# DeltaNet attention followed by a quick-GELU feed-forward block: the dummy matmuls around the first hops are laid out anew, and four key norms are multiplied in by another engine

## The chip, the cores and the metric

One core of one Trainium2 chip. The metric is the device time of one execution in microseconds (us); three executions are given by their median. One further execution was profiled. PE is TensorE, DVE VectorE, ACT ScalarE, POOL GpSimd, and SP the engine that issues most DMAs.

## The reference

```
# attention: B, H, S, D = 4, 8, 768, 48
k_n = k / (norm(k) + 1e-6)
for t in range(S):
    y[t]  = q[t] @ state
    v_old = k_n[t] @ state
    state = state + beta[t] * outer(k_n[t], v[t] - v_old)
# feed-forward: x is y as (3072, 384); w_in (384, 2048), w_out (2048, 384)
h = x @ w_in
g = h / (1 + exp(-1.702 * h))
out = g @ w_out
```

## The kernel before

**Units.** The sequence is cut into six chunks of 128 positions. A unit is one chunk of one of the four batches, with its eight heads; units are numbered chunk by chunk, so that 0 to 3 are the first chunk, 4 to 7 the second and 8 to 11 the third. Within a chunk the recurrence is solved in four blocks of 32 positions. For that each unit needs its keys turned (`turn`, L443: four PE transposes into psT, evacuated to kT), their Gram product (`gram`, L417: sixteen PE instructions into psG, evacuated to G), and the inverses of the 32 by 32 diagonal blocks (`invert`, L484: a long row of small DVE products, tiles P, YB and NT). The blocks of G go to DRAM (Nd) and come back as NT (`send_blocks`, `load_diagonals`); the inverse goes out as Yd and comes back as XB.

**Hops.** `together` (L938) does one hop for a pair of units: for each head, 32-row products with XB (`solve`, into psU) and with G (`below`, into psR). ACT copies psU to US, and DVE subtracts psR from V. A hop can start its psU when V of the hop before is updated. The first pair, units 0 and 1, has eight hops (0 to 7, loop L1118); the pair 2 and 3 has eight more (hop 0 at L1132, hops 1 to 7 in the loop at L1151). Beside the hops of the first pair the keys of units 6 and 7 are turned (hops 1 and 3) and their Gram products made (hops 4 and 5).

**Outputs.** `put_out(s)` (L1112) makes a unit's outputs (psY, sixteen products), the products for the state (psS), calls `fill(1.7)`, has DVE add psS to the state (tile ST), and lets ACT copy psY to xT and last. After an odd unit six transfers on SP's queue (xT<-last) complete xT. Only then can `hidden` (L737) start: x @ w_in into ph, in two PSUM banks shared with the dummies (tag moe), each evacuated by ACT's gelu into gT. `feed` does one piece of it.

**Dummies.** `warm(n)` (L137) issues n bf16 matmuls of 128 by 128 by 256 into a bank that nobody reads (ps_warm). Their counts are NW, NR, NA, NY and NU at L59. NY of them stand at the end of the first inverse (L550), in front of hop 0. In the hops of the first pair six follow hops 0, 1 and 3 and twelve follow hop 2; none stand at hops 4 and 5, where the Gram products are. Six stand in front of `put_out` of unit 1 (L1133), and twelve follow hops 1 and 2 of the second pair.

**Background work.** The weights arrive in a wide format, and each piece is made float32 by six operations, five on DVE and one (Relu) on ACT (`conversion`, L209). `background` (L296) is one generator: conversions of w_in, then `invert(1)`, then conversions of w_out, with the cost of each step written beside it. `fill(us)` (L307) takes steps from it until the written costs come to us. A finished piece can trigger further weight loads on SP's queue (`fetches`).

**Order.** vec, act, pe, pool and sync are wrappers that pin each operation in the order of the program text, so each engine and SP's queue works in that order. After the second pair a loop of 25 (L1185) does `fill(1.0)` and `feed()` each time and, at written points, steps of `prepare_early` (L1170) for units 8 to 11. That calls `normalize_mixed` (L335): ACT squares the keys, DVE sums them (ssq), POOL takes the root (rn), DVE adds 1e-6, takes the reciprocal and multiplies the keys by it in one operation. Two steps later the keys of units 8 and 9 are turned. Then `both_written` (L883) does g @ w_out (po) as pieces of w_out become ready, woven with the later chunks (`woven`, L985).

Of the kernel before, what the change touches and what calls it, by code (L numbers as in the profile page):

```python
# [12 lines left out]
ALU = mybir.AluOpType  # L13
ACT = mybir.ActivationFunctionType
# [4 lines left out]
def kernel(  # L19
# [21 lines left out]
    B, H, S, D = q.shape  # L41
# [9 lines left out]
    NB = C // BS  # L51
# [4 lines left out]
    HF, HM = FC // 2, DM // 2  # L56

    XR = DP - D
    NW, NR, NA, NY, NU = 80, 11, 3, 28, 12  # L59
    NQ = DFF // 4  # L60
    NPC = DFF // 8
    assert S % C == 0 and H == 8 and D <= DP and DM == H * D == KC * 128
# [57 lines left out]
    vec, act, pe, pool = Engine(nc.vector), Engine(nc.scalar), Engine(nc.tensor), Engine(nc.gpsimd)  # L120
# [16 lines left out]
    def warm(n, after=None):  # L137
        ps = ps_moe.tile([128, 256], F32, tag="moe", name="ps_warm")
        if after is not None:
            after(ps[:, 0:1], 0.0)  # L140
        for _ in range(n):
            pe.matmul(ps, lhsT=ones[:, 0:128], rhs=ones, start=True, stop=True)
# [164 lines left out]
    def fill(us):  # L307
        while us > 0:
            us -= next(behind, us)
# [6 lines left out]
    def home(n):  # L316
        return KX if n in (len(KN), 3 * B - 1) else KN[n % len(KN)]
# [17 lines left out]
    def normalize_mixed(n):  # L335
        K = home(n)[:, :, 0:D]
        ksq = wk.tile([128, H, D], F32, tag="ksq", name="ksq", bufs=1)
        act.activation(ksq, K, ACT.Square)
        yield
        ssq = wk.tile([128, H], F32, tag="ssq", name="ssq", bufs=4)  # L340
        vec.tensor_reduce(ssq, ksq, axis=AX.X, op=ALU.add)
        rn = wk.tile([128, H], F32, tag="rn", name="rn", bufs=4)
        pool.tensor_tensor(rn, ssq, half, op=ALU.pow)
        yield
        vec.tensor_scalar(rn, rn, 1e-6, None, op0=ALU.add)
        vec.reciprocal(rn, rn)
        vec.tensor_tensor(K, K, rn.broadcast_to([128, H, D]), op=ALU.mult)
        yield

    def normalize_first():  # L350
# [66 lines left out]
    def gram(n):  # L417

        c, b = units[n]
        kT = kTs[n]  # L420
        G = (
            g_tile().rearrange("p f (o t) -> p (f o) t", o=2) if n < HB
            else wk.tile([128, H, 128], F32, tag="G", name="G", bufs=6)
        )
        pool_, tag = (ps_seq, "seq") if c == 0 else (ps_big, "big")
        ps = [pool_.tile([128, NP, 128], F32, tag=tag, name="psG") for _ in range(2)]
        for h in range(H):
            r = slice(h % 2 * 64, h % 2 * 64 + D)
            pe.matmul(
                ps[h % 2][:, h // 2], lhsT=kT[r, h // 2, :], rhs=kT[r, h // 2, :],  # L430
                start=True, stop=True,
            )
        act.activation(G[:, 0::2], ps[0], ACT.Copy)
        if B <= n < 2 * B + HB:
            act.activation(G[:, 1::2], ps[1], ACT.Copy)
        else:
            vec.tensor_copy(G[:, 1::2], ps[1])
        ready[n] = KN[n % len(KN)], kT, G
        return G
# [3 lines left out]
    def turn(n):  # L443
        kTs[n] = wk.tile([128, NP, 128], F32, tag="kT", name="kT", bufs=5)
        transposed(home(n), kTs[n])
# [23 lines left out]
    def send_blocks(n, others=(), dma=sync):  # L469

        G = ready[n][2]
        Nd = dram.tile([H * C * BS], F32, tag="Nd", name="Nd", bufs=4)
        to = Nd.rearrange("(h p k) -> p h k", p=C, k=BS)
        for blk in range(NB):
            u = slice(blk * BS, (blk + 1) * BS)
            (beside if blk in others else dma)(out=to[u], in_=G[u, :, u])
        return Nd
# [95 lines left out]
    def bank(name, shape=(128, H, D)):  # L573
        return ps_seq.tile(list(shape), F32, tag="seq", name=name)
# [363 lines left out]
    def together(solves, belows):  # L938

        solves = [(X, blk) for X, blk in solves if X]  # L940
        belows = [(X, blk) for X, blk in belows if X]
        psU = bank("psU") if solves else None
        psR = bank("psR") if belows else None
        for h in range(H):
            for X, blk in solves:
                X.solve(blk, h, psU)
            for X, blk in belows:
                X.below(blk, h, psR)
        for X, blk in solves:
            X.solved(blk, psU)  # L950
        for X, blk in belows:
            X.rest(blk, psR)
# [159 lines left out]
    def put_out(s):  # L1112
        s.queries()
        s.outputs(True, lambda: fill(1.7))
        steps.pop(s.n)

    path, later = hops(*pair[:2]), hops(*pair[2:])
    for i in range(2 * NB):  # L1118
        together(*next(path))
        if i in (1, 3):  # L1120
            turn(B + HB + i // 2)
        if i in (4, 5):
            gram(B + HB + i - 4)
            Ndx.append(send_blocks(B + HB + i - 4))
        elif i < 2 * NB - 2:
            warm(NU if i == 2 else NU // 2)
        if 0 < i < 2 * NB - 1:
            fill(1.7)
        if i == 2 * NB - 2:
            put_out(pair[0])  # L1130
    load_diagonals(Ndx)
    together(*next(later))  # L1132
    warm(NU // 2)  # L1133
    put_out(pair[1])
    sync(out=KN[0], in_=KX)
    load(8, ((KN, k),), sync)
# [7 lines left out]
    def feed(n=1):  # L1144
        for _ in range(n):
            while ffn and next(ffn[0], None) is None:
                ffn.pop(0)
# [2 lines left out]
    ffn.append(hidden(xTs[0], gTs[0], slice(0, NTH), 1.3))  # L1150
    for i in range(1, 2 * NB):  # L1151
        together(*next(later))
        if i > 2:
            feed()
        else:
            warm(NU)
        fill(1.7)
    for s in pair[2:]:
        put_out(s)
# [10 lines left out]
    def prepare_early(n, gram_too=True):  # L1170

        for _ in normalize_mixed(n):
            yield
        yield
        if gram_too:
            turn(n)
            yield
            gram(n)
            Nds[n] = send_blocks(n)
            yield  # L1180
# [58 lines left out]
```

## Time and profile before

| what | value |
|---|---|
| three executions | 764.84, 770.88, 770.75 us |
| their median | 770.75 us |
| the profiled execution | 771.24 us |
| its span, first to last instruction | 769.5 us |
| its mean granted PE clock | 0.964 |
| clock by the page's slices of 19.2 us, the first nine, in tenths | 9 6 7 8 6 9 9 9 8 |
| dummies, number in all | 203 |
| psU before hop 0 starts | 65.11 us |
| first ph matmul after the wait for xT | 100.81 us |

All times within an execution count from its first instruction. Busy times of PE are modelled ends of pipelined matmuls. The granted clock is a share of full speed; in this trace it is 1.0 or 0.5. All lines of the kernel's engine operations carry the line of the pinning helper, L108, so rows are told apart by their tiles.

### The profile page before, as it was taken

The numbers are of one execution on the slowest core, as the hardware profiler recorded it, in microseconds if no ns is written. First come the engines' busy times: TensorE is split into PE (matmuls) and PEld (weight loads), VectorE is DVE, ScalarE is ACT, GpSimd is POOL, SyncE is SP. The second block draws the span as 40 slices with busy tenths as digits, with TensorE's granted clock in tenths as the row PEclk, the third lists the DMA queues.
The fourth block names the chain that finished last, engine by engine and source line by source line (L and its number), as shares of the span: only waits on it lengthen the run. The fifth ranks groups of instructions, "written<-read, shape, count | busy, mean of one in ns | idle before, by whom it ended". The sixth has DMA issues, their size and how long they took to land.

```text
span 769.5 us, 19639 instructions
## 1 busy us (share of the span) xinstructions
PE 729.1 (95%) x8427; PEld 625.3 (81%) x8427; DVE 489.3 (64%) x1014; ACT 238.7 (31%) x527; POOL 242.3 (31%) x210
## 2 busy tenths in 40 slices
PE   9288999988999999999999999999999999999998
PEld 7166868855667888898988898988988988988987
DVE  4798689999777676677677777767767850110000
ACT  3363443532333422322322323322322323222120
POOL 5023001310056541542632632722711601403122
PEclk9678699989999999999999999999999999999999
DMA  9985645541223113113113123113122120000000
GB/s 170 137 165 123 175 112 78 106 117 48 59 50 81 36 28 82 37 31 80 36 32 78 36 42 71 36 41 70 36 45 56 22 55 2 2 26 2 26 0 21
DMA packets 128182, 47.11 MB, mean 61 GB/s; under 512 B 117920, under 2 KB 122144, under 8 KB 128096
## 3 DMA queue, kind: packets, MB, share of 16 engines
q1 hardware_dynamic: 125568, 41.54, 26.3%
q0 software_dynamic: 1344, 3.93, 2.3%
q8 instruction: 66, 1.08, 0.6%
q10 hardware_dynamic: 1184, 0.39, 0.2%
q14 instruction: 20, 0.16, 0.1%
HBM read 33.13 MB, written 11.01 MB: 57 GB/s over the span
## 4 chain that ended last, share of the span: by engine, by line
PE 73%; DVE 16%; issue 3%; POOL 3%; DMA 3%; SPq 1%; ACT 0%; DVEq 0%; POOLq 0%; ACTq 0%
PE ph L108 27%; PE po L108 24%; PE psY L108 6%; PE psU L108 5%; DVE P L108 4%; DVE w_out L108 3%; PE psQ L108 3%; DVE YB L108 3%; PE psG L108 2%; PE ps_warm L108 2%; PE psR L108 2%; DVE NT L108 2%; PE psT L108 2%; DVE raw L108 1%; SPq L108 1%
## 5 line engine op out<-in xcount | busy, mean ns | idle before, releaser
L108 PE MATMUL ph<-xT,w_in 128*128 128x256 f32 x1152 | 262.9, 384 | 1.6 <-DMA xT<-last 1.4
L108 PEld LDWEIGHTS ph<-xT,w_in 128*128 128x128 f32 x1152 | 215.0, 190 | 33.3 <-issue 2.5
L108 PE MATMUL po<-w_out,gT 128*128 128x192 f32 (+1 forms) x736 | 147.5, 354 | 3.9 <-DVE o L108 3.6
L770 POOL TENSOR_TENSOR gT<-gT 128x512 f32<-128x512 f32 x80 | 106.3, 1337 | 122.9 <-ACT gT L108 112.3
L108 PEld LDWEIGHTS po<-w_out,gT 128*128 128x128 f32 x736 | 121.4, 191 | 19.7 <-DVE o L108 4.6
L108 DVE TENSOR_TENSOR V<-V,psR 64x384 f32<-64x384 f32 (+1 forms) x96 | 53.3, 556 | 129.1 <-PE psR L108 127.9
L108 ACT ACTIVATE gT<-ph 128x512 f32<-128x512 f32 x92 | 54.9, 596 | 146.5 <-PE ph L108 146.4
L108 DVE TENSOR_TENSOR P<-NT,YB 64x2 f32<-64x2 f32 (+9 forms) x200 | 94.0, 470 | 6.2
L108 DVE TENSOR_REDUCE YB<-P 64x2 f32<-64x2 f32 (+9 forms) x200 | 81.8, 409 | 6.9
L108 PEld LDWEIGHTS psU<-V,XB 32*32 32x32 f32 x1536 | 59.8, 108 | 30.0 <-issue 15.9
L108 ACT COPY US<-psU 32x384 f32<-32x384 f32 x92 | 43.1, 469 | 129.5 <-PE psR L108 122.8
L108 PE MATMUL po<-TW,gT 128*128 128x192 f32 x480 | 83.0, 328 | 0.0
L108 PEld LDWEIGHTS po<-TW,gT 128*128 128x128 f32 x480 | 77.9, 190 | 1.1 <-issue 0.3
L108 PE MATMUL psU<-V,XB 32*32 32x48 f32 x1536 | 70.4, 207 | 5.5 <-DVE V L108 3.0
L108 DVE TENSOR_TENSOR o<-o,po 128x192 f32<-128x192 f32 x40 | 13.5, 351 | 75.8 <-PE po L108 75.3
L108 PE MATMUL psR<-US,G 32*32 32x48 f32 x2016 | 55.8, 205 | 3.6 <-ACT US L108 3.6
L639 POOL TENSOR_SCALAR_AFFINE_SELECT M<-M 128x1024 f32<-128x1024 f32 x19 | 23.5, 1236 | 95.0 <-DVE M L108 62.1
L108 PEld LDWEIGHTS psR<-US,G 32*32 32x32 f32 x2016 | 47.2, 106 | 4.6 <-ACT US L108 4.3
L108 DVE TENSOR_TENSOR P<-NT 64x512 f32<-64x512 f32 (+7 forms) x50 | 44.9, 898 | 2.0
L93 POOL DMA_DIRECT2D KN<-in_k_dram x12 | 11.5, 958 | 81.6 <-PE psY L108 81.6
L108 DVE TENSOR_REDUCE NT<-P 64x32 f32<-64x512 f32 (+9 forms) x50 | 33.4, 668 | 1.7
L108 PE MATMUL psQ<-QS,kT 48*128 48x176 f32 (+1 forms) x368 | 33.7, 324 | 0.8 <-ACT QS L108 0.7
(122 smaller groups left out, 762.8 us busy)
## 6 DMA issues: line engine op xcount, KB each, us to landing
V<-in_v_dram SPq DMA_DIRECT2D x24, 192.0 KB, 3.2
out_dram<-o SPq DMA_DIRECT2D x24, 192.0 KB, 2.8
QP<-in_q_dram SPq DMA_DIRECT2D x22, 192.0 KB, 3.4
raw<-in_moe_w_out_dram SPq DMA_DIRECT2D x9, 384.0 KB, 3.9
NT<-Nd SPq DMA_DIRECT2D x24, 128.0 KB, 3.0
XB<-Yd SPq DMA_DIRECT2D x24, 128.0 KB, 3.1
Yd<-NT SPq DMA_DIRECT2D x22, 128.0 KB, 2.2
Nd<-G SPq DMA_DIRECT2D x86, 32.0 KB, 1.7
```

The lines of the kernel that those rows point to most:

```text
L93: dma(out=place(dst, n)[:, :, 0:D], in_=src[b, :, c * C : (c + 1) * C, :].rearrange("h p d -> p h d"),)
L108: return lambda *a, **kw: tc.keep_in_program_order(op(*a, **kw))
L639: (pool if self.n < B else nc.gpsimd).affine_select(out=self.M, in_=self.M, compare_op=ALU.is_gt, fill=0.0, base=0, pattern=[[0, H], [1, 1 ...
L770: (engine or nc.gpsimd).tensor_tensor(o, a, b, op=op)
```

## The change

The number of dummies in front of hop 0 of the first pair goes from 28 to 38. After hops 0, 1 and 3 there are eight instead of six; after hops 4 and 5, beside the Gram products, eight instead of none; hop 2 keeps twelve. In front of unit 1's outputs `fill(1.9)` takes the place of six dummies. In the second pair six dummies are added after hop 3, in front of its piece of ph; those after hops 1 and 2 keep their number and still stand ahead of the fill. In `normalize_mixed` the one DVE multiplication of a unit's keys by the reciprocal becomes eight ACT activations, one for each head, with the reciprocal as their scale.

```diff
-    NW, NR, NA, NY, NU = 80, 11, 3, 28, 12
+    NW, NR, NA, NY, NU = 80, 11, 3, 38, 12
...
         vec.tensor_scalar(rn, rn, 1e-6, None, op0=ALU.add)
         vec.reciprocal(rn, rn)
-        vec.tensor_tensor(K, K, rn.broadcast_to([128, H, D]), op=ALU.mult)
+        for h in range(H):
+            act.activation(K[:, h], K[:, h], ACT.Copy, scale=rn[:, h : h + 1])
...
         if i in (4, 5):
             gram(B + HB + i - 4)
             Ndx.append(send_blocks(B + HB + i - 4))
-        elif i < 2 * NB - 2:
-            warm(NU if i == 2 else NU // 2)
+        if i < 2 * NB - 2:
+            warm(NU if i == 2 else 2 * NU // 3)
         if 0 < i < 2 * NB - 1:
             fill(1.7)
         if i == 2 * NB - 2:
             put_out(pair[0])
     load_diagonals(Ndx)
     together(*next(later))
-    warm(NU // 2)
+    fill(1.9)
     put_out(pair[1])
...
     for i in range(1, 2 * NB):
         together(*next(later))
+        if i < 4:
+            warm(NU if i < 3 else NU // 2)
         if i > 2:
             feed()
-        else:
-            warm(NU)
         fill(1.7)
```

## The prediction

> **What bounds the kernel now.** I read the page's busy rows first, then the tables by stage, then each engine's order of time. The whole says little: PE is busy 95% of the span. The change lies between 59 and 157 us, so the question is what ends the waits there.
>
> ```profile
> span 769.5 us, 19639 instructions
> PE 729.1 (95%) x8427; PEld 625.3 (81%) x8427; DVE 489.3 (64%) x1014; ACT 238.7 (31%) x527; POOL 242.3 (31%) x210
> ```
>
> By stage (PE, PEld, DVE, ACT and POOL busy, granted clock, DMA share, GB/s), DVE has under 2 us idle in each of the 32 and 35 us after 125, and PE is full until 157 and then idle for 5.87 us. So DVE (conversion of the weights, inverses, V updates) is the bound up to 192, and PE behind it: time that DVE gains before 192 is worth its face value as long as PE has that 5.87 us to give.
>
> ```profile
> 125.00:157.00 32.00, 32.00 (x183) 26.99 (x181) 30.18 (x62) 15.53 (x30) 8.69 (x5) 1.00 0.63 115
> 157.00:192.00 35.00, 29.13 (x276) 18.12 (x275) 33.48 (x77) 9.86 (x21) 4.16 (x3) 0.90 0.27 75
> ```
>
> Next the clock. Cut at the edges where it changes (3.41 us apart or a multiple), the table for PE alone gives busy time, granted clock, DMA share and GB/s:
>
> ```profile
> 65.29:68.70 3.41, 2.37 (x87) 1.00 0.81 126
> 68.70:72.11 3.41, 3.41 (x74) 0.50 0.46 71
> 72.12:75.53 3.41, 3.41 (x83) 1.00 0.91 236
> 75.53:78.94 3.41, 2.34 (x73) 1.00 1.04 172
> 78.95:82.36 3.41, 3.41 (x54) 0.50 0.73 159
> 89.19:92.60 3.41, 3.41 (x28) 0.50 0.83 233
> 99.42:102.83 3.41, 2.02 (x53) 1.00 0.77 155
> 102.84:106.25 3.41, 3.41 (x30) 0.50 1.01 292
> ```
>
> A stretch with PE busy for 2.0 to 2.4 us of 3.41, much of it 32-row products, is followed by half clock; one that holds twelve dummies (92.60 on) is not. Six stretches are at 0.50 here (78.95 to 92.60 is four of them), 20.5 us.
>
> Last the order of time of PE, DVE, SP's queue and ACT (start, duration, count, idle before and its releaser):
>
> ```profile
> 65.11 0.86 PE L108 MATMUL psU<-V,XB 32*32 32x48 f32 x16 [1.37 <-DMA XB<-Yd]
> 89.40 1.46 PE L108 MATMUL ps_warm<-ident 128*128 128x256 bf16 x6
> 90.79 1.96 PE L108 MATMUL psY<-M,US 128*64 128x128 f32 x16
> 100.81 1.10 PE L108 MATMUL ph<-xT,w_in 128*128 128x256 f32 x4 [1.40 <-DMA xT<-last]
> 93.25 0.36 DVE L108 TENSOR_TENSOR ST<-psY,ST 128x192 f32<-128x192 f32 x1 [4.42 <-PE psY L108]
> 127.69 0.56 DVE L108 TENSOR_TENSOR KN<-KN,rn 128x384 f32<-128x384 f32 x1
> 88.53 4.73 SPq L108 DMA_DIRECT2D NT<-Nd x4
> 94.04 4.58 SPq L108 DMA_DIRECT2D xT<-last x6
> 49.46 3.72 ACT L108 ACTIVATE KN<-KN,TW 128x48 f32<-128x48 f32 x16
> 127.73 0.60 ACT L108 ACTIVATE gT<-ph 128x512 f32<-128x512 f32 x1 [1.99 <-PE ph L108]
> ```
>
> The reader is to see DVE's 4.42 us hole at 93.25, in which it waits for unit 1's outputs, and the six dummies at 89.40 ahead of them; and, just behind, SP's queue, which has the NT loads until 93.26 and only then xT.
>
> **The change part by part.** The profiled execution took 771.24 us, its span 769.5; the median of the three runs is 770.75, 0.49 less. I sum against the profiled one.
>
> *Ten more dummies in front of the hops.* At full clock one is 1.28/12 = 0.107 us (twelve from 93.94 to 95.22), so ten are 1.07 us. The 28 end at 63.74, and psU waits for XB until 65.11: the 1.37 us hide them, cost 0. With that cover gone, or the clock at half there, ten cost 2.13, that is 0.76 on the path. I take 0: the clock rose at 61.88.
>
> *Two more at hops 0, 1 and 3.* Hop 0 is followed by a 1.04 us wait for the second XB and hop 3 by 0.40 for V: hidden (0.21 each). Hop 1 is at half clock and PE runs through to psU: 2 x 0.21 = 0.43 on the path.
>
> *Eight beside each Gram product (hops 4 and 5).* 0.86 each at full clock, 1.70 at half. After hop 4 PE waits 0.67 for V, which leaves 0.2. At hop 5 the sixteen Gram instructions take 2.08 at half clock (80.14); at full 1.16 (76.98), so 1.16 + 0.86 = 2.02: nothing, if the clock holds. Does it? The stretch from 75.53 has three dummies and one Gram product; it gains nearly eight, 0.84 us, which lifts PE from 2.34 to about 3.2. I take it that the clock holds through 79 to 82 and is lost again in the outputs (85.8 on), which have only small products.
>
> *Six fewer in front of unit 1's outputs, and `fill(1.9)` there.* psY starts at 90.86 and could at 89.47: 1.39 off PE's path, 0.64 at full clock. The fill puts some 1.9 us of conversion into DVE's hole. Queued behind it on DVE is the ST add; ACT's xT copies come after that add (93.64, after 93.25), then SP's xT transfers, then ph. With psY earlier, DVE is what ends last: it stands at 88.83 now, about 0.4 earlier or later by the hops, and 1.9 more puts the add near 90.5 instead of 93.25.
>
> *What is late next.* SP. Its order is fixed, xT<-last behind NT<-Nd, and the last NT load is issued at 92.96 because it waits for the landing of Nd behind 1.5 MB of w_out. So xT goes out at about 93.3 instead of 94.04 and ph starts 0.75 us earlier, not 2.7; the hops behind ph on PE's queue too. The hole of DVE moves to about 99, before hop 4 of units 2 and 3. What is left is 1.9 us of conversion done ahead, plus a time gain between 0 (PE goes cold while it waits for xT and does its first ph at half clock) and 0.75; I take 0.5. Sum for DVE: 2.4.
>
> *Six dummies at hop 3 of the later pair.* They lie in the wait for xT (1.40 us, longer afterwards): 0.64, or 1.28 at half clock, hidden. The twelve at hops 1 and 2 only change place.
>
> *Norms of keys 8 to 11 on ACT.* DVE loses four multiplies of 0.56 us, but each overlaps its follower (127.69 to 128.16 is 0.47): 4 x 0.47 = 1.9 to 2.2, I take 2.1. ACT gains 4 bursts of eight. The sixteen at 49.46 take 3.72 us, so a burst takes 1.86 by this row. ACT stands before them until DVE's reciprocal; behind them in its queue are the gelu that frees ph's bank, the conversions' Relu and G. Two banks of ph give 2.56 - 0.60 = 1.96 us of slack, and ACT is idle 1.99 before the gelu at 127.73: hidden. For keys 10 and 11 (150.97, 154.43) kT, G and Relu stand close, and I charge DVE 0.1; between 0 and 4 x 1.86.
>
> The Trainium skill ("ScalarE: Activation LUTs", Rules for kernel authors) says the opposite of this edit, to multiply on VectorE, and budgets about 0.3 us per ACTIVATE plus 0.83 ns per element: an estimate by that page of 8 x 0.34 = 2.7 us a burst, 0.7 over the slack, so 2.9 us for four and a sum of 769.7. The trace agrees with 0.34 as the duration of one (339 ns), but they start 0.23 us apart.
>
> **Sum.** 2.4 + 2.1 - 0.1 = 4.4 us off DVE up to 192 (hop 1's 0.43 is inside the 2.4, since DVE then has less of a hole). PE can follow: 5.87 us idle after 157. Behind 192 PE is busy 568 of 578 us and starts earlier. 771.24 - 4.4 = 766.8; at the level of the median, 770.75 - 4.4 = 766.4.
>
> **Rivals.**
> *The clock holds through and SP keeps up.* For it: dummies in every stretch. Then DVE's holes at 72.41, 83.71, 93.25 and 106.70 close: 0.21 + 0.87 + 4.42 + 1.36 = 6.9, plus 2.1, less 0.5 of dummies: 8.5, and 762.3. Against: SP at 92.96.
> *The dummies do not change the clock.* Then hop 5's cost 1.70 and hop 4's 0.2, hop 1's 0.43, less 1.39: the add comes 0.94 later, and 1.9 - 0.94 + 2.1 leaves 3.1: 767.7. The Trainium skill ("TensorE: Matmul & The Clock Gate", Why this matters for your kernels) ties the drop to PE-idle gaps of over some 3 us. By that rule dummies beside work that has no such gap change nothing. The trace disagrees on the cause: the longest gap from 75.53 to 78.94 is 0.67 us and the clock fell.
> *PE becomes the bound.* One or two more half-clock stretches between 157 and 192, where there were two (167.7 to 174.5), take 1.7 us of PE each: the gain falls to about 1, and 769.8.
> *ACT's bursts are felt in full (the other side).* Each burst is in front of a Relu or gelu for which DVE or PE waits: 7.4 us, less 4.4: 3.0 slower, 773.8. It decides once ACT is more than 1.96 us late; against it stands ACT's 15.5 us busy of 32.
>
> **How the numbers follow.** My forecast 0.45; the clock holds 0.17; no change of clock 0.20; PE the bound 0.10; ACT 0.08. Predicted 766.4. The range goes from the second case, 762.0, to beyond PE as the bound, 771.0; ACT's case and the tails are the 2 in 10 outside. A measurement of this kernel tells 1%, 7.7 us, from no change: faster by more than that is below 763.0, most of the clock case, 0.15; slower, above 778.5, only ACT's far end, 0.05; within, 0.80.
>
> **What would show it.** The 0.50 stretches between 78.95 and 85.8 at 1.00; the ST add near 90.5; xT<-last at 93.3 and ph near 100; KN<-KN,rn gone from DVE and 32 activations of about 0.23 us spacing on ACT; the idle of 3.64 us before psR at 169.17 gone. I am wrong if ph starts before 99, if DVE waits on ACT's Relu between 140 and 157, or if PE has no idle left after 157 while DVE has.

## The result, and the profile after

| kernel | executions | median us | range us | median granted clock |
|---|---|---|---|---|
| before | 20 | 770.68 | 764.84 to 774.48 | 0.964 |
| changed | 20 | 766.58 | 765.14 to 768.51 | 0.975 |

The ratio is 0.9954, 95% interval 0.9939 to 0.9969: 4.1 us less by the medians, where 4.4 were forecast. (The clock of before is the median of 35 executions in a later group.) The profiled execution took 767.01 us.

```profile
span 765.2 us, 19731 instructions
PE 727.6 (95%) x8459; PEld 624.0 (82%) x8459; DVE 487.3 (64%) x1010; ACT 245.5 (32%) x559; POOL 240.3 (31%) x210
PEclk9568999989999999999999999999999999999999
```

Busy times are within 2 us of those of before, but for ACT, which has 32 instructions more; in the clock's row the fifth slice of 19 us is 9 where it was 6.

The sum came out, and its terms did not. To see it, the execution has to be cut where DVE's inverses begin and end, since the first inverse ends by chance at 58.63 in one profile and at 56.69 in the other, in code that nobody changed. These are DVE's rows in order of time, before and then changed: the memset that ends the first inverse, the first and the last operation of the second (NT with bI), the first of the third.

```profile
58.63 0.06 DVE L108 MEMSET ps_warm<- 128x1 f32 x1
111.73 1.22 DVE L108 TENSOR_TENSOR NT<-NT,bI 128x1024 f32<-128x1024 f32 x1
139.66 1.22 DVE L108 TENSOR_TENSOR NT<-YB,bI 128x1024 f32<-128x1024 f32 x1
180.79 1.21 DVE L108 TENSOR_TENSOR NT<-NT,bI 64x1024 f32<-64x1024 f32 x1
```

```profile
56.69 0.06 DVE L108 MEMSET ps_warm<- 128x1 f32 x1
105.31 1.22 DVE L108 TENSOR_TENSOR NT<-NT,bI 128x1024 f32<-128x1024 f32 x1
132.62 1.23 DVE L108 TENSOR_TENSOR NT<-YB,bI 128x1024 f32<-128x1024 f32 x1
176.86 1.21 DVE L108 TENSOR_TENSOR NT<-NT,bI 64x1024 f32<-64x1024 f32 x1
```

The hops took 53.10 us and take 48.62: 4.48 gained, where I had 2.4. The second inverse took 27.93 and takes 27.31: the multiply of key 8 is gone from it. From its end to the third inverse it was 41.13 and is 44.24: 3.11 lost, in a stage where I had written 1.5 us of gain. The lost part is most of what the hops had won; the rest of the execution is the same to 0.4 us (588.75 and 588.37). So of the 4.3 us between the spans of these two profiles 1.94 lie in front of the change, by chance, and only 2.4 behind it: the gain of 4.1 rests on the medians of twenty executions each, and not on this pair.

In the hops, cut at the edges of the clock (PE busy, granted clock, DMA share, GB/s):

```profile
73.11:76.52 3.41, 2.58 (x66) 1.00 1.04 180
76.52:79.93 3.41, 3.41 (x70) 1.00 0.79 132
79.94:83.35 3.41, 2.76 (x59) 1.00 0.51 108
83.35:86.76 3.41, 2.12 (x55) 1.00 1.00 349
86.76:90.17 3.41, 3.16 (x55) 0.50 0.78 201
90.18:93.59 3.41, 3.41 (x138) 1.00 0.18 53
```

One stretch is at half clock instead of six. It follows 83.35 to 86.76, where unit 0's outputs and 32-row products are and no dummy is. The chain that I had followed reads so now, for PE, DVE and SP:

```profile
65.34 0.86 PE L108 MATMUL psU<-V,XB 32*32 32x48 f32 x16
89.85 0.36 DVE L108 TENSOR_TENSOR ST<-psY,ST 128x192 f32<-128x192 f32 x1
90.64 4.43 SPq L108 DMA_DIRECT2D xT<-last  x6
95.87 1.53 PE L108 MATMUL ph<-xT,w_in 128*128 128x256 f32 x6
```

DVE has no wait in front of the ST add (4.42 us before). xT goes out at 90.64, straight behind ACT's copies, and ph starts at 95.87 without any idle of PE: SP was not late. (Of every difference from a time of before, 1.94 us are the front's.) In the later stage the columns are PE, PEld, DVE, ACT and POOL busy:

```profile
125.00:157.00 32.00, 30.42 (x170) 24.41 (x168) 28.10 (x55) 21.14 (x57) 7.08 (x5) 1.00 0.50 103
157.00:192.00 35.00, 30.76 (x318) 19.35 (x318) 31.77 (x78) 10.33 (x22) 2.74 (x2) 0.90 0.29 84
```

ACT went from 15.53 to 21.14 us of 32, and DVE now idles for 3.9 us there. The changed kernel is some 7 us further in its work at 125, so the two tables do not cover quite the same; from the second inverse's end to the third's start, cut as above, DVE is idle for 1.71 of 41.13 us before and for 5.47 of 44.24 now, with ACT busy for 17.76 and 24.30. DVE's waits from 125 to 192 (us, times, longest) were 0.6 in all before, and are:

```profile
DVE w_out L108 <- ACT w_out L108: 2.5, 4, 1.3
DVE V L108 <- PE psQ L108: 0.9, 3, 0.6
DVE w_out L108 <- DMA w_out<-in_moe_w_out_dram: 0.8, 1, 0.8
DVE rn L108 <- POOL rn L108: 0.2, 1, 0.2
```

The reader is to see the first row: DVE stands before the third step of a conversion until ACT has done its Relu. ACT's order of time shows what is ahead of one such Relu, with DVE's wait for it below:

```profile
146.16 1.91 ACT L108 ACTIVATE KN<-KN,rn 128x48 f32<-128x48 f32 x8 [0.19 <-DVE rn L108]
147.98 0.57 ACT L108 ACTIVATE kT<-psT 128x512 f32<-128x512 f32 x1
148.46 0.92 ACT L108 ACTIVATE w_out<-w_out,low 128x768 int32<-128x768 int32 x1
```

```profile
149.41 0.96 DVE L108 SCALAR_TENSOR_TENSOR w_out<-w_out 128x768 int32<-128x768 int32 x1 [0.67 <-ACT w_out L108]
```

Not every one of the four waits stands right behind a burst. The longest, 1.27 us at 140.44, is for a Relu (139.80) that has other work of ACT just ahead of it, among it a gelu that had waited 1.99 us for PE. What the bursts are worth in all is therefore left to e12.

### The profile page after: what moved, and what is told of

Same layout as the page of the kernel before. It is cut to its first block, busy times and chain, and to the rows that moved or that the text cites. A ratio compares the mean times of both kernels' runs of the same rounds, so it can differ in the third digit from the quotient of the medians.

```text
span 765.2 us, 19731 instructions
## 1 busy us (share of the span) xinstructions
PE 727.6 (95%) x8459; PEld 624.0 (82%) x8459; DVE 487.3 (64%) x1010; ACT 245.5 (32%) x559; POOL 240.3 (31%) x210
## 3 DMA queue, kind: packets, MB, share of 16 engines
q0 software_dynamic: 1344, 3.93, 2.2%
## 4 chain that ended last, share of the span: by engine, by line
PE 78%; DVE 10%; issue 3%; ACT 3%; POOL 3%; DMA 2%; SPq 1%; DVEq 0%; POOLq 0%; ACTq 0%
PE ph L108 28%; PE po L108 25%; PE psY L108 5%; PE psU L108 5%; PE psQ L108 4%; PE psG L108 3%; PE ps_warm L108 3%; PE psT L108 2%; PE psR L108 2%; DVE w_out L108 2%; DVE P L108 2%; DVE YB L108 1%; POOL TW L771 1%; DVE V L108 1%; ACT KN L108 1%
## 5 line engine op out<-in xcount | busy, mean ns | idle before, releaser
L108 PEld LDWEIGHTS po<-w_out,gT 128*128 128x128 f32 x736 | 121.5, 191 | 20.5 <-DVE o L108 4.6
L108 ACT COPY US<-psU 32x384 f32<-32x384 f32 x92 | 43.3, 470 | 130.1 <-PE psR L108 122.0
L108 PEld LDWEIGHTS psU<-V,XB 32*32 32x32 f32 x1536 | 57.0, 105 | 27.6 <-issue 13.2
L108 PE MATMUL psU<-V,XB 32*32 32x48 f32 x1536 | 67.5, 203 | 3.4 <-DVE V L108 2.7
L108 PE MATMUL ps_warm<-ident 128*128 128x256 bf16 x235 | 33.9, 302 | 1.4 <-POOL low L108 1.4
```

Of the source, the lines that this page charges most:

```text
L108: return lambda *a, **kw: tc.keep_in_program_order(op(*a, **kw))
```

## The experiments

Theory A was the prediction's sum: the fill brings 1.9 us of work done ahead and some time, the norms on ACT 2.0, the dummies mostly hold their own price. Theory B came from the trace after: the dummies bring the hops 4 to 5 us through the clock, and the norms on ACT bring nothing, since what DVE saves it waits for. Twelve kernels ran, in three groups of four; each ratio is to the kernel before on the same chip, with its 95% interval. Each kernel has six (e7) to twelve executions. The ratio is not the quotient of the two medians, and the two can differ: e1's medians alone would give 0.9929.

| run | what differs | median us | ratio | interval |
|---|---|---|---|---|
| e1 | changed, norms on DVE | 765.05 | 0.9956 | 0.9925 to 0.9986 |
| e2 | before, norms on ACT | 769.87 | 0.9986 | 0.9967 to 1.0004 |
| e3 | before, fill for the six dummies | 768.07 | 0.9973 | 0.9956 to 0.9991 |
| e4 | changed, 28 dummies at the front | 767.06 | 0.9958 | 0.9938 to 0.9978 |
| e5 | changed, no dummies at the Gram products | 767.98 | 0.9976 | 0.9948 to 1.0005 |
| e6 | dummies alone | 765.97 | 0.9939 | 0.9911 to 0.9967 |
| e7 | changed, norms on POOL | 764.39 | 0.9915 | 0.9886 to 0.9943 |
| e8 | changed, only key 8 on ACT | 765.62 | 0.9934 | 0.9910 to 0.9958 |
| e9 | changed, again | 766.96 | 0.9979 | 0.9959 to 0.9999 |
| e10 | dummies, norms on POOL, no fill | 765.91 | 0.9957 | 0.9935 to 0.9980 |
| e11 | changed, bursts of sixteen | 773.20 | 1.0045 | 1.0021 to 1.0068 |
| e12 | changed, four multiplies left out | 764.64 | 0.9932 | 0.9906 to 0.9957 |

The three groups' medians of before are 770.49 (e1 to e4), 770.04 (e5 to e8) and 769.66 (e9 to e12). From each profile the same cuts on DVE as above give the stages: hops, from the first inverse's end to the second's start, and "between", from the second's end to the third's start. Half clock is counted from the first psU of hop 0 to the second inverse's start.

| profile | hops us | half clock in them | between us |
|---|---|---|---|
| before | 53.10 | 20.5 | 41.13 |
| changed; e9 | 48.62; 47.41 | 3.4; 3.4 | 44.24; 44.32 |
| e1 | 46.75 | 0 | 42.36 |
| e2 | 47.95 | 6.8 | 41.88 |
| e3 | 51.92 | 27.3 | 42.28 |
| e4 | 47.01 | 3.4 | 44.65 |
| e5 | 48.14 | 10.2 | 44.95 |
| e6 | 47.77 | 0 | 41.17 |
| e7 | 46.24 | 0 | 43.30 |
| e8 | 50.98 | 17.1 | 42.56 |
| e10 | 48.87 | 0 | 41.35 |
| e11 | 46.22 | 0 | 50.92 |
| e12 | 48.60 | 3.4 | 41.99 |

Each row is one execution, and how much half clock it has is partly chance: e2 has the dummies of before and drew 6.8, e8 those of the changed kernel and drew 17.1. That is why the medians decide, and the stages explain.

The column "between" also shows that not all of the 3.11 us lost there is the norms'. With the fill and the norms on DVE it is 42.28 (e3) and 42.36 (e1), some 1.2 more than without the fill (41.13 before, 41.17 in e6), and less is left to do behind it (588.08 and 588.06 us from the third inverse's start, against 588.75 and 589.79). The norms on ACT add the rest, 1.9 us from e1 to the changed kernel.

**e1, the norms back on DVE.**

```diff
-        for h in range(H):
-            act.activation(K[:, h], K[:, h], ACT.Copy, scale=rn[:, h : h + 1])
+        vec.tensor_tensor(K, K, rn.broadcast_to([128, H, D]), op=ALU.mult)
```

> The changed kernel with the four key norms multiplied by DVE again, as before; dummies and fill as changed. Theory A (the prediction's sum): the norms on ACT are worth 2.0 us, so without them 768.6, ratio to before 0.997, and DVE has no wait on ACT's Relu. Theory B (read from the trace after: the lead of DVE at the end of the second inverse is about 7 us, and 2.5 us of it goes in waits for ACT's Relu behind the norm bursts): the norms on ACT are worth nothing or cost something, so without them 765.5 to 766.8, ratio 0.993 to 0.995, and the DVE waits on ACT between 133 and 157 fall from 2.5 to under 0.6 us.

765.05 and not 768.6; DVE's waits for ACT's w_out fell to 0.2 us. By the median that is B, though the ratio's interval still holds 0.997: eight of twelve executions lie at or under 766.1 and four between 768.4 and 773.0. Their clock is lower, 0.969 to 0.973, on the mean 0.970 against 0.9765 for the eight; by the slope worked out under e6 that is worth 2.5 of the 6.5 us that they are longer on the mean. The rest is open.

**e2, the norms on ACT alone** (the reverse edit, in the kernel before).

> The kernel before with only the norms of keys 8 to 11 on ACT. Theory A: 2.0 us faster, 768.7, ratio 0.9974. Theory B: within 0.7 us of before, 770 to 771.4, ratio 0.999 to 1.001, with DVE waiting for ACT's Relu by about as much as the four multiplies took.

0.6 us faster by the medians; the interval holds both no change and A's 0.9974. Alone it does not decide. DVE waited 2.4 us for a Relu in its profile, in one wait.

**e3, the fill alone.**

```diff
-    warm(NU // 2)
+    fill(1.9)
     put_out(pair[1])
```

> The kernel before with only the six dummies in front of unit 1's outputs replaced by fill(1.9). Theory A: 1.9 us of work done in DVE's hole plus up to 0.75 of time, so 2.4 faster, 768.3, ratio 0.997. Theory B (the clock does most): 0.5 to 2 us faster, since the hops before it still run at half clock, 768.7 to 770.2, ratio 0.9975 to 0.9995.

768.07: A's number by the median, and outside B's by little; the interval holds both. By the median the fill is worth in the kernel before what I gave it.

**e4, 28 dummies at the front.**

```diff
-    NW, NR, NA, NY, NU = 80, 11, 3, 38, 12
+    NW, NR, NA, NY, NU = 80, 11, 3, 28, 12
```

> The changed kernel with 28 dummies in front of hop 0 instead of 38. Theory A: the ten are hidden behind the wait for XB, and fewer change little: 766.6 plus or minus 0.7, ratio 0.995 to 0.9965. Theory B1: the ten keep the clock up through hops 0 and 1, so without them half clock is back between 65 and 72 and the time is 1 to 2 us longer, 767.6 to 768.6. Theory B2: in the trace after, the 38 end at 65.3 while XB could be there at about 63, so they cost up to 2 us and without them it is 764.6 to 766.

767.06, in A's range (765.9 to 767.3), with an interval that reaches B1's: no effect shown. In the changed kernel's profile the 38 run to 65.34 with psU right behind them, 8.65 us after the end of the first inverse, and DVE then waits 3.93 us for the first psR; in e4's profile psU waits 1.1 us for XB, starts after 7.00, and DVE waits 2.29. So in that execution the dummies were on the path. Of the ten profiles with 38 only e12's has the same two numbers (8.63 and 3.93); in the others psU starts after 6.4 to 7.5. By the medians the ten neither cost nor buy anything that can be measured.

**e5, no dummies at the Gram products.**

```diff
-        if i < 2 * NB - 2:
+        if i < 2 * NB - 2 and i not in (4, 5):
             warm(NU if i == 2 else 2 * NU // 3)
```

> The changed kernel without the sixteen dummies beside the Gram products of hops 4 and 5. Theory C (the clock in the hops is what the dummies buy): the half clock of 79 to 93 comes back in most executions, the mean granted clock falls from 0.975 to 0.968 or less, and the time rises by 1 to 3 us over the changed kernel, to 767.6 to 769.6. Theory D (the fill does it, the dummies there are padding): the clock may fall, the time stays at 766.6 plus or minus 0.8.

767.98 with a median clock of 0.971 instead of 0.975: in C's range by the time, and halfway by the clock. The interval reaches 1.0005 and overlaps the changed kernel's, so the 1.4 us are likely and not shown. What the profile shows is the return of the half clock behind the two hops (PE busy, clock):

```profile
77.16:80.57 3.41, 2.21 (x54) 1.00 0.64 143
80.58:83.99 3.41, 2.69 (x44) 0.50 0.70 173
83.99:87.40 3.41, 3.41 (x52) 0.50 1.01 333
87.40:90.81 3.41, 3.41 (x48) 0.50 0.53 146
```

**e6, the dummies alone** (norms on DVE, six dummies for the fill).

> The changed kernel with its dummies, but with six dummies instead of the fill in front of unit 1's outputs, and the norms on DVE. Theory C: the clock alone closes most of DVE's hole by making psY earlier, so 767 to 768.3, 2.4 to 3.7 faster than before. Theory D: the dummies alone bring at most 1 us, 769.5 to 770.5.

765.97, faster than both theories had, and as fast as the whole change. Its clock is 0.978, and its profile has no half clock in the hops. So the dummies by themselves bring some 4 us, to which I had given 0.5 together with the time of the fill. The executions of the kernel before point the same way without any edit. Over the 93 of them in the three groups, time and granted clock go together (correlation -0.79), with 0.39 us less for each 0.001 of clock; from 0.964 to 0.975 that is 4.3 us.

**e7, the norms on POOL.**

```diff
-        for h in range(H):
-            act.activation(K[:, h], K[:, h], ACT.Copy, scale=rn[:, h : h + 1])
+        pool.tensor_tensor(K, K, rn.broadcast_to([128, H, D]), op=ALU.mult)
```

> The changed kernel with the four norms multiplied by POOL, in one operation each, so that neither DVE nor ACT has them. Theory B (ACT's bursts eat what DVE gains): DVE saves its 2 us and its waits for ACT's Relu stay under 0.6, so 763.5 to 765.5, faster than the changed kernel by 1 to 3. Theory A (the bursts cost 0.1): the same as the changed kernel, 766.0 to 767.2.

764.39, the lowest median of the study: 5.65 us under before, and under the changed kernel by 2.2. That is in B's range, though DVE's waits for ACT's Relu are 0.7 and not under 0.6. It is not shown to be faster than leaving the norms on DVE: e1's interval overlaps. POOL does one in 0.83 to 1.43 us. That is not free for DVE: from the second inverse's end to the third's start DVE is busy for 39.96 us here and for 38.82 in e12, which has the same operations on DVE and no multiply on POOL. At 138.25, beside POOL's multiply at 138.00, the third step of a conversion took 0.99 us and not 0.55. The waits of DVE from 125 to 192:

```profile
DVE V L108 <- PE psQ L108: 1.2, 3, 0.9
DVE w_out L108 <- ACT w_out L108: 0.7, 2, 0.5
DVE rn L108 <- POOL rn L108: 0.7, 2, 0.5
```

**e8, key 8 alone on ACT.**

```diff
+        if n == 2 * B:
             for h in range(H):
                 act.activation(K[:, h], K[:, h], ACT.Copy, scale=rn[:, h : h + 1])
+        else:
+            vec.tensor_tensor(K, K, rn.broadcast_to([128, H, D]), op=ALU.mult)
```

> The changed kernel with only the norm of key 8 on ACT, where DVE is in the second inverse and no Relu is queued; keys 9 to 11 on DVE. Theory B: better than all four on ACT by 0.5 to 2, 764.6 to 766.1. Theory A: three multiplies come back to DVE, 1.5 us slower than the changed kernel, 768.1.

765.62. A's 768.1 would be 0.9975 and lies outside the interval: three multiplies back on DVE do not cost what A charged. B's range holds it.

**e9, the changed kernel again.**

> The changed kernel as it is, beside the other three of this group on one chip. 766.0 to 767.2, ratio 0.994 to 0.997 to before, by every theory.

766.96 and 0.9979: within the expectation by the median, but outside it by the ratio (0.994 to 0.997), which is less favourable than in the first group (0.9954); the intervals overlap.

**e10, POOL norms without the fill.**

> The dummies of the changed kernel, norms on POOL, and six dummies instead of the fill in front of unit 1's outputs. Theory A (the fill's 1.9 us of work done ahead adds to the rest): 1.9 slower than with fill and POOL norms (764.4), so 766.3. Theory E (where the clock holds, psY comes early enough that the hole the fill was for is mostly gone): within 0.7 of it, 763.8 to 765.1.

765.91, nearer to A: with the fill it was 764.39, so by the medians the fill is worth about 1.5 also where the clock holds. The two intervals overlap (0.9935 to 0.9943), the runs are of different groups, and the like pair with the norms on DVE, e1 and e6, gives 0.9 us by the medians and the other sign by the ratios (0.9956 and 0.9939): this is not settled. E falls by its number: DVE still waited 1.4 us for psY here. The work that the fill does ahead turns up after the third inverse begins: from there to the end it is 589.96 us, and 588.13 in e7 (589.79 in e6 and 588.06 in e1).

**e11, each burst doubled.**

```diff
-            act.activation(K[:, h], K[:, h], ACT.Copy, scale=rn[:, h : h + 1])
+            for s in (slice(0, D // 2), slice(D // 2, D)):
+                act.activation(K[:, h, s], K[:, h, s], ACT.Copy, scale=rn[:, h : h + 1])
```

> The changed kernel with each key norm as sixteen activations of 24 columns instead of eight of 48, which makes each of the four bursts on ACT about 1.6 to 1.9 us longer. Theory B (bursts for keys 9 to 11 lie in front of Relus that DVE waits for): 2 to 5 us slower than the changed kernel, 768.5 to 771.5, and DVE waits for ACT's Relu between 60 and 192 rise from 2.5 to 6 or more. Theory A (bursts are hidden by the 1.96 us of slack in ph's banks, and only the part over it is felt): under 1 us slower, 766.6 to 767.6.

773.20, 6.2 over e9 beside it: more than B had. Four bursts became 3.39 - 1.90 = 1.49 us longer each, 6.0 in all, so nearly every microsecond of burst beyond the first 1.9 is paid. ACT and DVE's waits from 125 to 192:

```profile
140.65 3.38 ACT L108 ACTIVATE KN<-KN,rn 128x24 f32<-128x24 f32 x16
```

```profile
DVE w_out L108 <- ACT w_out L108: 10.0, 5, 2.7
DVE w_out L108 <- DMA w_out<-in_moe_w_out_dram: 1.4, 1, 1.4
```

**e12, the multiplies left out.**

```diff
-        for h in range(H):
-            act.activation(K[:, h], K[:, h], ACT.Copy, scale=rn[:, h : h + 1])
```

> The changed kernel with the multiplication of keys 8 to 11 by the reciprocal left out altogether (these keys stay without their norm; the rest is computed). It bounds what moving the multiplies can bring. Theory B: 1.5 to 2.5 us faster than the changed kernel, 764.0 to 765.1, the same as with POOL. Theory A: the same as the changed kernel within 0.5, since it has them at 0.1.

764.64, 2.3 under e9, as B had it, and no better than POOL's 764.39. Having the norms on ACT costs 2.3 us against not having them at all. Its profile agrees with the changed kernel's to 0.02 us up to the second inverse's end (48.60 and 27.31) and then needs 41.99 where that needs 44.24. DVE's waits for ACT's Relu are 0.8 in place of 2.5, so 1.7 of the 2.5 are the bursts'. The longest wait, 1.27 us there, is 0.5 here. With e11 this shows that the bursts on ACT are paid for in DVE's waits.

## Why the prediction was right in the sum and wrong in two steps

- **The bound.** Right as far as it went: DVE and its queue partners end the waits between 59 and 192, and the rest moves with them (588.75 and 588.37 after the third inverse's start).
- **The dummies and the clock: mechanism right, size wrong.** I had the half clock gone from 79 to 86 and back in the outputs; it came back at 86.76, which is 88.70 on the scale of before. But I charged the dummies their price and let almost none of the gain through, because I held ph back by SP's queue. The hops gained 4.48 us in the profile, and e6, which has the dummies alone, has 4.1 by its median against 0.5 in my sum. The term that failed is "what is late next": the NT loads that I took as fixed, the last at 92.96, moved up with the rest of SP's queue: the last went out at 89.29, 3.67 us earlier, of which 1.94 are the front's. Counted from the end of the first inverse, xT goes out 1.46 us earlier and the sixth ph matmul ends 2.6 us earlier (40.7 for 43.3), where I had 0.75 for both. Nor did the wait for XB always hide the ten dummies that I had at 0 (e4). In some profiles PE does wait for xT afterwards, by 0.4 to 1.5 us (e7, e10), so SP is close, but not a wall. That is half of the rival in which the clock holds and SP keeps up (762.3); its hops came, and its norms did not. That the dummies raise the clock and shorten the time is shown by e6; by what rule the clock falls is not (last section).
- **The fill.** 1.9 of work and 0.5 of time: e3 measured 2.4 alone, by its median. The ST add stands at 89.85, where I put it near 90.5, but the nearness is luck: counted from the end of the first inverse it is at 33.2 us, and I had 31.9. What the fill is worth beside the dummies is not settled (e10).
- **The norms: wrong.** I gave them 2.1 - 0.1 = 2.0 us. By the medians they are worth 0.6 alone (e2, whose interval does not exclude 2.0) and nothing beside the dummies (e1, e8), and against no multiply they cost 2.3 (e12). The four multiplies are gone from DVE, as said, and 32 activations start 0.23 us apart. The step that failed is "hidden": I compared a burst of 1.86 with a slack of 1.96 in ph's two banks, one burst at a time. I had seen that kT, G and Relu stand close to the bursts of keys 10 and 11, and charged 0.1. DVE needs the Relu sooner than PE needs its bank: with bursts longer by 1.49 each the time rose by 6.2 (e11), so past the first 1.9 us of a burst there is next to no slack towards ACT. The rival had this mechanism, priced at four full bursts; 1.7 us of waits of DVE came.
- **By the Trainium skill's rule** ("ScalarE: Activation LUTs", Rules for kernel authors: multiply on VectorE) the edit was the wrong way, and I set it aside for its price of a burst. The trace agrees with me on the price (1.90 and not 2.7), and with the Trainium skill in that DVE does the same multiplication in 0.56 us and that moving it brought nothing (e1).
- **Too much and too little cancel.** That the sum came out is luck. Of the two wrong terms one was some 2 us short (4.5 in the hops for 2.4) and the other some 2 us generous. A forecast that hits the time by 0.2 us can be wrong in half of its terms, and only runs like e6 and e12 tell.
- **Smaller readings.** The 769.7 that the prediction sets beside its sum stands on the level of the profiled execution; on that of the forecast it is about 769.2. No row has the end of twelve dummies at 95.22; their starts, 93.94 for the first and 94.94 for the tenth, give 0.11 us for one.
- **What I had said would show me wrong** did in part. DVE waited for Relu between 140 and 157. The other sign, ph before 99, came too (95.87), but it was badly chosen: before, two matmuls of ph had run at 98.73, and the row at 100.81 is of the four behind the wait for the rest of xT. And one sign that I had counted on stayed away. PE's wait before psR is as long as it was (3.64 before), since ACT's copy of US and PE both come about 3.2 us earlier:

```profile
166.02 0.45 PE L108 MATMUL psR<-US,G 32*32 32x48 f32 x8 [3.69 <-ACT US L108]
```

## What to carry to other kernels

Where the granted clock changes within the stage, cut the trace at the edges of the clock before pricing anything else, and ask what the stretches ahead of half clock have in common; a few microseconds of dummy work in the right stretch can be worth more than moved work. Before work is moved to an engine that is idle half the time, look at what is queued behind it there and who waits for that: an in-order queue passes a burst on to everyone behind it. Here POOL, for which DVE waited only 0.7 us, was by the medians a better home than ACT by 2.2 us, even though it takes 0.83 to 1.43 us where DVE took 0.56; that it is better than leaving the work on DVE is not shown. And when stages differ in their limits, check the terms stage by stage, since a right total says little about them.

## What the runs showed of the hardware that was not expected

- **When the clock falls.** In the changed profile the clock survived a stretch with 2.58 us of PE busy in 3.41 that held eight dummies, and one with 2.76, and fell after 2.12; in e5 it fell after 2.21, and in the kernel before after 2.34 and 2.37. The Trainium skill ("TensorE: Matmul & The Clock Gate", Why this matters for your kernels) gives idle gaps of over some 3 us as the cause. The longest wait of PE in e5's profile between 60 and 90 is 0.8 us, so no such gap is needed here. (Where there is one, 3.69 us before psR at 166.02 in the changed profile, the clock fell too: the stretch from 161.86 has 0.48 us busy, and half clock follows it.) But the busy share of a stretch does not decide it alone. The clock fell after 2.75 us in e8 (63.23 to 66.64), in a stretch with eight dummies, and held after 1.87 in e7 (84.71 to 88.12), in one with none. Nor does a full stretch always bring full clock back: before, PE was busy for all 3.41 us from 78.95, and the next stretch stayed at half. Which products count, and over how long a time, was not tried. So it is shown that the added dummies raise the clock, and not by what rule.
- **The spread is mostly the clock's.** With the dummies the executions lie within 3.4 us of each other in the first group (765.14 to 768.51), where before they spread over 9.6; in the later groups the time of before goes with its clock, at a correlation of -0.79 (e6). The edges of the clock fall elsewhere in each execution, and with the dummies fewer of them seem to matter. e1's four late executions show that this is not the only source.
- **Small activations.** Eight of 128x48 take 1.90 us and sixteen of 128x24 take 3.39: halving the columns leaves the spacing at 0.21 to 0.23 us, so in such a burst the number of instructions is what costs.
